# Seven products for two more experts, and a written order of steps: a linear-attention and expert-mix kernel on one core

## The chip, the core and the metric

The kernel runs on one core of a Trainium2 chip. The time is the device time of one execution in microseconds (us), as the median of the runs. A profile is one further execution, taken by the hardware profiler; its rows are in microseconds from the start of the span.

Engines: TensorE (PE in the profile, its weight loads PEld), VectorE (DVE), ScalarE (ACT), GpSimd (POOL), and SyncE (SP), which only issues transfers. GpSimd issues transfers too.

## What is computed

Four sequences (B = 4) of 768 steps, 8 heads of 48. First a linear attention with a decaying state, then a mix of four experts over the 3072 tokens with 8 x 48 = 384 features:

```python
f = 1.0 / (1.0 + np.exp(-f_logit))
for t in range(S):
    state = f[:, :, t, :, None] * state + np.einsum('bhd,bhe->bhde', k[:, :, t], v[:, :, t])
    y[:, :, t] = np.einsum('bhd,bhde->bhe', q[:, :, t], state)
...
p = domain_probs / (domain_probs.sum(-1, keepdims=True) + 1e-09)
for e in range(E):                       # E = 4, w1[e]: 384 x 1024, w2[e]: 1024 x 384
    h = np.maximum(x @ w1[e], 0.0)
    out += p[:, e:e + 1] * (h @ w2[e])
```

## The kernel before

**Chunks and halves.** The 768 steps are cut into six chunks of 128 (c = 0 to 5). A chunk holds 4 x 128 = 512 tokens, four token tiles, one for each batch b. Attention of a chunk runs batch by batch: the gates (`gate1`, `gate2`, ScalarE), the prefix sum of the log gates as a matmul (`cs`, in chunk 0 also `cq`), exponentials (`exps`, `expq`, ScalarE), products with q and k (`q`, `k`, VectorE or GpSimd), transposes (`tpq`, `tpk` on TensorE and their eviction `ev_tp`, or `tp` by DMA), the scores (`at`), masked on their way out of PSUM (`ev_at0`, `ev_at1`; two of them copied by ScalarE and masked by GpSimd, `mask1`), the output (`y`), the state's update (`kv`, `ev_kv`, then four `sf` on GpSimd), and the transposed output as the experts' input (`xt`, `ev_xt`).

**The experts.** In chunk 0 and the first half of chunk 1, experts run one by one over unweighted tokens: `h c.e.fc.n0` is a block of the first matrix product (`mm_h`), `relu` its ReLU, `o c.e.nt.half` half of the second product for a token tile (`mm_o`, L502: 4 matmuls of 384 columns), and `ev_o` adds it, times the token's share p, to the output tile `o` (VectorE, or ScalarE for expert 0). From the second half of chunk 1 on, experts go in pairs over weighted tokens (`hs`, `relu_s`), half a chunk (256 tokens) at a time, and the second product is done with **seven products** in place of eight: each of the three operands is split into 2 x 2 blocks (token tile, half of the 1024, half of the 384 columns), sums of blocks of `h` (`s1` to `s4`, L541) and differences of blocks of `w2` (`t 1`, `t 2`, `t 4` into `ts_sb`, and `t 3` in place, L561) are made on VectorE, and seven block products (`p c.hf.pair.m`, `mm_p`, L574: 8 matmuls of 192 columns each for a pair) are evicted and added into `o` (`ev_p`, 192 columns). Functions for one expert alone exist as well (`add_p1`, L825, `mm_p1`, L583, `s_sum1`, L555, `ev_p1`, L591); `BLOCKED = ()` (L1029) says that no expert uses them.

**Weights and loads.** GpSimd issues the loads of the weights, which are converted to 16 bits on the way, in 11 pieces (`w issue 0` to `w issue 10`): four halves of the first matrices of experts 0 and 1, two halves of expert 0's second matrix, then whole matrices: expert 2's first (6), expert 1's second (7), expert 3's first (8), expert 2's second (9), expert 3's second (10). The last waits for the load of k of chunk 1 (L306). It also issues the loads of v of chunk 0. All other loads, stores and DMA transposes are issued by SyncE in one queue. The loads of f of chunk 1 wait for weight pieces 6 and 8.

**What sets the order.** Every step is an `Op` with a cost for each engine that can run it, a priority, dependencies, and the buffers that it takes and frees (8 PSUM banks among them). `Plan.run` (L92) goes through a modelled time: whenever an engine is free, it takes the step of best priority that is ready then and there; so the plan picks both the order and, where a step has two costs, the engine. `MOVES` (L15) shifts the priorities of 157 steps and pins some of them to an engine. The instructions are then emitted in that order, and on the chip every engine runs its own list in order, waiting on semaphores.

**Fillers.** Where the modelled time leaves TensorE a gap up to the first `h`, matmuls on a constant tile fill it, into a spare PSUM bank that nothing reads (L1011 and L1022):

```python
o.pad, t = int(gap / 0.42) if t < 7.0 else int((gap - 0.5) / 0.25) if gap > PADGAP else 0, o.end
...
for _ in range(o.pad):
    nc.tensor.matmul(out=spare, lhsT=busy[:, 0:128], rhs=busy, start=True, stop=True)
```

In this kernel there are ten: six in front of `cs 0.0`, four in front of the first transposes (`tpk 0.1`).

**The end.** In the last pair of the last half chunk (`TAIL`) products come in an order of their own, so that stores can start early; product 3, the last of the seven as they are set up, is followed by the store of columns 192 to 384 of one token tile.

Of the kernel before, what the change touches and what calls it, by code (L numbers as in the profile page):

```python
# [14 lines left out]
MOVES = (  # L15
    "ld f0.0=-1085.4;ld k0.0=-996.5;ld q0.0=-995;ld f0.1=-1063.1;ld k0.1=-1011.8;ld q0.1=-997;ld f0.2=-1016.8;ld k0.2=-1048.4;"
    "ld q0.2=-166.9;ld q1.2=24.6;expq 0.0=17.8;cs 0.0=-15.3;cq 0.1=51.7;ev_tp 0.1=-2353.3@DVE;cq 0.3=-31.8;cs 0.3=-127.3;"
    "tpq 0.3=51.9;ev_at0 0.2=-26.8;y 0.2=4;ld p=3.1;cs 1.0=11.5;q 1.1=30.5;v 1.1=56.8@POOL;q 1.2=50.2;cs 1.3=270.6;"
    "ev_xt 1.0=136.7@ACT;ev_ys 1.2.1.1=4.6@DVE;ev_at1 1.3=-207.2;y 1.3=51.7;sf 1.0.2=13;sf 1.0.3=26.9;ld f2.0=-181.4;ld k2.2=8.7;"
    "ld q2.2=14.3;h 0.1.3.0=45.1;relu 0.1.3.0=-71.4@DVE;o 0.0.2.0=34;ev_o 0.0.2=-57.7@DVE;h 0.2.2.0=48.5;o 0.1.1.0=31.2;"  # L20
    "o 0.1.2.0=56.8;h 0.2.6.0=186.9;h 0.3.1.0=69.5;o 0.2.0.1=61.7;o 0.2.1.0=88.9;h 0.3.4.0=93.3;o 0.2.3.0=70.7;ev_at0 2.1=-7.7;"
    "ev_at1 2.1=-87.3;ev_ys 2.1.1.0=129.8@ACT;ev_at1 2.3=121.4;ld f3.0=-26.9;ld k3.0=0.1;ld f3.2=21.5;ld q3.2=20;o 0.3.0.0=50.1;"
    "o 0.3.1.1=16.7;o 0.3.3.0=-27.2;o 0.3.3.1=95;store 0.3.0=69.5;h 1.0.3.0=3.1;h 1.1.2.0=49;h 1.2.3.0=37.5;o 1.1.1.1=63.6;"
    "h 1.2.4.0=53.4;h 1.2.5.0=37.4;h 1.2.6.0=-29.2;o 1.2.0.0=200.4;h 1.3.1.0=57.8;h 1.3.2.0=67.2;store 1.0.0=14.5;"
    "hs 1.1.0.0.6=35.5;s3 1.1.0=243.4;s4 1.1.0=217.3;hs 1.1.1.0.0=175.5;ev_at0 3.1=-16.6;kv 3.0=99.1;ev_kv 3.1=47.6;ld f4.2=12;"
    "ld k4.2=23.5;hs 2.0.0.0.0=9.8;p 1.1.1.1=2.1;hs 2.0.0.0.2=-36.6;relu_s 2.0.0.0.2=-20.8@DVE;p 1.1.1.6=5.4;hs 2.0.0.1.2=-24.8;"
    "ev_p 1.1.1.7=144.7;store 1.2.0=28.9;s1 2.0.0=96.7;s3 2.0.0=-259.2;hs 2.0.1.0.0=200.7;hs 2.0.1.1.0=-150.7;hs 2.0.1.0.2=9.8;"
    "relu_s 2.0.1.1.2=-62.7;hs 2.1.0.1.4=3.4;p 2.0.1.3=4;store 2.1.0=51.8;s2 2.1.0=24.1;p 2.1.0.2=159;ev_p 2.1.0.6=-167.6@DVE;"
    "hs 2.1.1.0.4=263.3;tp 4.0=22.8;cs 4.1=7.4;tp 4.2=66.2;ev_at1 4.0=69.6;y 4.1=27.9;ev_ys 4.1.1.0=101.9@DVE;ev_kv 4.3=7.7;"
    "ld f5.0=27.4;ld q5.0=202.1;ld v5.0=-19.4;ld k5.2=-47.3;p 2.1.1.1=11.5;p 3.0.1.1=16.2;hs 3.1.0.1.0=11.7;p 3.0.1.2=7.9;"  # L30
    "s2 3.1.0=75.8;s3 3.1.0=-2.8;hs 3.1.1.1.0=28.1;hs 3.1.1.0.2=26.6;hs 3.1.1.1.2=7.1;hs 3.1.1.0.6=17.4;p 3.1.0.4=88.2;"
    "hs 3.1.1.1.6=-14.6;cs 5.2=10.5;cs 5.3=83.5;at 5.3=22.9;hs 4.0.0.0.0=134.5;p 3.1.1.1=27.9;p 3.1.1.5=117.6;p 3.1.1.4=5;"
    "s1 4.0.0=1.2;hs 4.0.1.0.0=55.6;hs 4.0.1.1.0=171.1;hs 4.0.1.1.2=-25.1;p 4.0.0.5=76.5;hs 4.0.1.0.4=-17.7;hs 4.1.0.1.2=30.5;"
    "p 4.0.1.5=11.3;hs 4.1.1.0.2=39.4;hs 5.0.0.1.0=207.4;ev_p 4.1.1.5=-27.2;hs 5.0.0.1.4=109.2;hs 5.0.1.1.2=46.5;hs 5.0.1.0.4=11.8;"
    "hs 5.0.1.1.4=19.4;hs 5.0.1.0.6=-25.9;p 5.0.0.4=30.3;p 5.0.1.6=542.6;hs 5.1.0.1.2=33.6;p 5.0.1.5=26.4;s1 5.1.0=41.9;"
    "hs 5.1.1.0.0=32.3;hs 5.1.1.1.2=28.8;hs 5.1.1.0.4=85.1;p 5.1.0.7=87.1;p 5.1.1.2=890.3"
)


class Op:  # L40


    def __init__(self, name, costs, emit, prio, deps=(), takes=(), frees=(), lag=0.0):
        self.name, self.costs, self.emit, self.prio = name, costs, emit, prio
        self.deps = [d for d in deps if d is not None]
        self.takes, self.frees, self.lag = list(takes), list(frees), lag
        if name.split(" ")[-1].startswith("0.") and {"ACT", "DVE"} & set(costs):
            self.lag += 0.1
        self.end = self.start = self.engine = None
        self.pad = 0  # L50
        self.port, self.turn = False, None


class Plan:
# [4 lines left out]
    def __init__(self, rooms):  # L59
        self.moves = dict(m.split("=") for m in MOVES.split(";") if m)  # L60
# [3 lines left out]
    def add(self, *args, **kw):  # L64
        op = Op(*args, **kw)
        by, _, engine = self.moves.get(op.name, "0").partition("@")
        op.prio += float(by)
        if engine:
            op.costs = {engine: op.costs[engine]}
        op.port = op.name[0] in "qkvs" and op.name[:2] not in ("kv", "st") and "issue" not in op.name or op.name[:2] == "t "  # L70
        self.ops.append(op)
# [20 lines left out]
    def run(self):  # L92
        for o in self.ops:
            for k in o.frees:
                self.left[k] = self.left.get(k, 0) + 1
        left = sorted(self.ops, key=lambda o: o.prio)
        free_at = {e: 0.0 for o in left for e in o.costs}
        free_at.update({"DMA": 0.8, "DVE": 5.0, "POOL": 3.5, "ACT": 2.1, "PE": 2.0})
        freeing, done, now, port = [], [], 0.0, 0.0
        while left:  # L100
            for f in [f for f in freeing if f[0] <= now + 1e-9]:
                freeing.remove(f)
                self.rooms[f[1]].append(f[2])
            for e in ("PE", "ACT", "DVE", "POOL", "DMA"):
                while free_at[e] <= now + 1e-9:
                    for o in left:
                        if e in o.costs:
                            t = self.ready(o, e)
                            if t is not None and t <= now + 1e-9 and self.take(o):
                                break  # L110
                    else:
                        break
                    left.remove(o)
                    o.engine, o.start = e, now
# [4 lines left out]
                    for k in o.frees:  # L119
                        self.left[k] -= 1  # L120
                        if self.left[k] == 0:
                            freeing.append((o.end + self.LATENCY + (o.lag if e == "DMA" else 0.0), k[0], self.slot[k]))
                    done.append(o)
            nexts = [t for t in free_at.values()] + [f[0] for f in freeing]
            for o in left:
                for e in o.costs:
                    nexts.append(self.ready(o, e) or 0.0)
            nexts = [t for t in nexts if t > now + 1e-9]
            if left and not nexts:
                raise RuntimeError("no step can run: " + ", ".join(o.name for o in left[:8]))  # L130
            if left:
                now = min(nexts)
# [4 lines left out]
def kernel(  # L137
# [95 lines left out]
    for nm, a in (("f", f_logit), ("q", q), ("k", k), ("v", v)):  # L233
# [7 lines left out]
        "ys": ([T, 2, HD], BF16), "xT": ([128, KD, NT], BF16), "xs": ([128, 2, KD, TH], BF16),  # L241
# [7 lines left out]
    alias = {"xT": "x", "xs": "x", "hs": "h", "ys": "yb", "praw": "o"}  # L249
# [51 lines left out]
    def load_w(i, e, which, ks, cols):  # L301
# [4 lines left out]
        if i == w_last:  # L306
# [254 lines left out]
    def t_sum(e, j):  # L561
        b = lambda kh, cols: w2_sb[:, e, half_k(kh), cols]
        t = lambda i: ts_sb[:, e, i - 1]
        o, in0, in1 = {1: (t(1), b(0, HI_), b(0, LO_)), 2: (t(2), b(1, HI_), t(1)), 4: (t(3), b(1, LO_), t(2)),
                       3: (b(0, HI_), b(1, HI_), b(0, HI_))}[j]
        return nc.vector.tensor_tensor(out=o, in0=in0, in1=in1, op=ALU.subtract)

    def factors(m, e, blk, s):
# [3 lines left out]
                7: lambda: (s(3), w(0, HI_))}[m]()  # L572

    def mm_p(c, hf, p, m, bank, first):  # L574
        out_ = tl("mp", c, hf, p, bank)[:, 0:DH]
# [388 lines left out]

    for e in BLOCKED:
        t_sums(e)
# [104 lines left out]
```

## Time and profile before

| | |
|---|---|
| median of 3 runs | 287.11 us (286.66 to 287.74) |
| profiled execution | 287.44 us, of it 285.7 us span |
| TensorE busy | 277.4 us, 3016 matmuls |
| VectorE, ScalarE, GpSimd busy | 196.1, 180.6, 114.1 us |
| transfers | 41.85 MB, mean 146 GB/s |

The span goes from the first to the last instruction; the execution's own time is 1.7 us longer. Matmuls are pipelined: the length printed for a group holds the drain of its last one, so the price of one is taken from the start of a group to the start of the next. A busy row in the view by stretches gives start and end, length, then busy time and number of instructions of TensorE, its weight loads, VectorE, ScalarE and GpSimd, then the granted TensorE clock, the busy share of the DMA engines and GB/s.

### The profile page before, as it was taken

What the parts mean: (1) busy time and instruction counts of PE and PEld (TensorE: products, weight loads), DVE (VectorE), ACT (ScalarE), POOL (GpSimd) and SP (SyncE); (2) the same over time, 40 slices, a digit from 0 to 9 for tenths busy, and PEclk for the clock granted to TensorE, in tenths of its full rate; (3) what the DMA queues carried; (4) which work ended last, traced back from release to release, by engine and by line L of the source; (5) the groups of instructions that cost most, each with busy time, mean ns of one, the idle gap of its engine ahead of it and who ended that gap; (6) DMA issues with size and microseconds to landing.
All of it is one profiled execution on the core that took longest, in us unless ns stands there. A gap on an engine that the chain in (4) does not pass through costs nothing.

```text
span 285.7 us, 7476 instructions
## 1 busy us (share of the span) xinstructions
PE 277.4 (97%) x3016; PEld 236.7 (83%) x3020; DVE 196.1 (69%) x402; ACT 180.6 (63%) x336; POOL 114.1 (40%) x186
## 2 busy tenths in 40 slices
PE   6889999999999999999999999999999999999995
PEld 4667555657877999999999998999899998999994
DVE  5794144697779896875888848886888730874374
ACT  6768756568657963586668766658638348836710
POOL 5999101528663760866036756343750000000000
PEclk9999999999999999999999999999999999999999
DMA  6999999999977999999879999989675210050003
GB/s 157 214 199 207 208 192 205 178 202 178 183 142 151 160 197 155 210 184 185 178 150 189 164 224 210 144 191 158 74 164 107 57 55 2 19 122 31 2 0 110
DMA packets 153687, 41.85 MB, mean 146 GB/s; under 512 B 144029, under 2 KB 152861, under 8 KB 153653
## 3 DMA queue, kind: packets, MB, share of 16 engines
q1 hardware_dynamic: 142404, 34.66, 65.0%
q0 software_dynamic: 11248, 6.72, 16.3%
q8 instruction: 23, 0.38, 0.6%
q14 instruction: 12, 0.09, 0.1%
HBM read 31.51 MB, written 4.72 MB: 127 GB/s over the span
## 4 chain that ended last, share of the span: by engine, by line
PE 78%; DMA 14%; POOL 5%; SPq 1%; issue 0%; DVE 0%; POOLq 0%
PE ps_m L521 33%; PE ps_m L580 29%; DMA w_sb<-in_moe_w_dram 10%; PE ps_m L504 6%; PE ps_m L489 4%; DMA k<-in_k_dram 4%; POOL w_sb L303 2%; PE ps_m L428 2%; PE ps_m L455 1%; POOL vb L284 1%; PE ps_m L451 1%; PE ps_m L338 1%; PE ps_m L461 1%; POOL AT L432 1%; SPq L290 1%
## 5 line engine op out<-in xcount | busy, mean ns | idle before, releaser
L521 PE MATMUL ps_m<-x,w_sb 128*128 128x256 bf16 x864 | 104.8, 273 | 0.0
L529 ACT ACTIVATE h<-ps_m 128x512 bf16<-128x512 f32 x111 | 66.2, 598 | 46.1 <-PE ps_m L521 38.8
L521 PEld LDWEIGHTS <-w_sb 128*128 128x128 bf16 x864 | 82.9, 98 | 9.4
L580 PEld LDWEIGHTS <-S 128*128 128x128 bf16 x576 | 48.7, 98 | 0.9
L607 DVE TENSOR_TENSOR o<-ps_m,o 128x192 f32<-128x192 f32 x91 | 31.3, 354 | 22.0 <-PE ps_m L580 21.0
L580 PEld LDWEIGHTS <-h 128*128 128x128 bf16 x432 | 36.2, 98 | 0.6
L504 PE MATMUL ps_m<-w_sb,h 128*128 128x384 bf16 x192 | 35.3, 326 | 0.4 <-DMA w_sb<-in_moe_w_dram 0.4
L489 PE MATMUL ps_m<-x,w_sb 128*128 128x128 bf16 (+2 forms) x260 | 34.5, 281 | 0.6 <-DMA w_sb<-in_moe_w_dram 0.4
L411 ACT ACTIVATE yb<-ps_m,pn 128x384 bf16<-128x384 f32 x54 | 28.1, 584 | 7.7 <-PE ps_m L455 6.4
L476 POOL TENSOR_TENSOR Sf<-Sf,egs 48x192 f32<-48x192 f32 x40 | 21.0, 526 | 27.1 <-DVE Sf L468 17.4
L444 DVE TENSOR_TENSOR AT<-ps_m,mask 128x512 bf16<-128x512 f32 x40 | 25.2, 683 | 8.6 <-PE ps_m L428 8.5
L500 ACT ACTIVATE h<-ps_m 128x512 bf16<-128x512 f32 (+1 forms) x42 | 22.5, 536 | 12.8 <-PE ps_m L489 11.8
L489 PEld LDWEIGHTS <-w_sb 128*128 128x128 bf16 x264 | 21.7, 98 | 9.5 <-DMA w_sb<-in_moe_w_dram 0.6
L544 DVE TENSOR_TENSOR S<-h 128x1024 bf16<-128x1024 bf16 x36 | 25.2, 713 | 6.1 <-ACT h L529 5.5
L580 PE MATMUL ps_m<-ts_sb,S 128*128 128x192 bf16 x288 | 29.2, 246 | 0.0
L580 PE MATMUL ps_m<-w_sb,S 128*128 128x192 bf16 x288 | 28.7, 246 | 0.0
L504 PEld LDWEIGHTS <-h 128*128 128x128 bf16 x192 | 18.3, 98 | 12.5 <-DMA w_sb<-in_moe_w_dram 0.9
L388 POOL TENSOR_TENSOR qk<-q,e 128x384 bf16<-128x384 f32 x19 | 22.7, 1205 | 14.5 <-ACT e L371 9.7
L580 PE MATMUL ps_m<-w_sb,h 128*128 128x192 bf16 x288 | 28.0, 246 | 0.0
L527 DVE TENSOR_SCALAR h<-ps_m 128x512 bf16<-128x512 f32 x33 | 22.4, 691 | 8.1 <-PE ps_m L521 7.5
L371 ACT ACTIVATE e<-ps_m 128x384 f32<-128x384 f32 x40 | 23.4, 704 | 5.8 <-PE ps_m L338 5.4
L388 POOL TENSOR_TENSOR qk<-k,e 128x384 bf16<-128x384 f32 x20 | 20.2, 1016 | 16.7 <-PE ps_m L580 7.4
(87 smaller groups left out, 317.5 us busy)
## 6 DMA issues: line engine op xcount, KB each, us to landing
out_dram<-o SPq DMA_DIRECT2D x23, 192.0 KB, 2.3
w_sb<-in_moe_w_dram POOLq DMA_DIRECT2D x5, 768.0 KB, 16.3
k<-in_k_dram SPq DMA_DIRECT2D x10, 384.0 KB, 5.6
q<-in_q_dram SPq DMA_DIRECT2D x10, 384.0 KB, 5.2
v<-in_v_dram SPq DMA_DIRECT2D x10, 384.0 KB, 5.4
f<-in_f_logit_dram SPq DMA_DIRECT2D x9, 384.0 KB, 4.6
w_sb<-in_moe_w_dram POOLq DMA_DIRECT2D x6, 384.0 KB, 8.6
f<-in_f_logit_dram SPq DMA_DIRECT2D x6, 192.0 KB, 3.7
```

The lines of the kernel that those rows point to most:

```text
L371: nc.scalar.activation(out=o, in_=i, func=AF.Exp, scale=1.0 if j else -1.0)
L388: return engines[eng].tensor_tensor(out=tl("qk", c, b)[:, j, :, 0:D].rearrange("t (i r) d -> t i r d", r=2), in0=tl("qk"[j], c, b // 2)[:, ...
L411: nc.scalar.activation(out=ys, in_=y, func=AF.Copy, scale=pe)
L444: nc.vector.tensor_tensor(out=tl("AT", c, b)[:, r].rearrange("s i t -> s (i t)"), in0=tl("A", c, b, r).rearrange("s i t -> s (i t)"), in1= ...
L489: nc.tensor.matmul(out=hp(c, e, fc, n0, n1, nf)[:, f], lhsT=w1_sb[:, e, kk, (fc + f) * 128:(fc + f + 1) * 128], rhs=tl("xT", c)[:, kk, n0: ...
L500: nc.scalar.activation(out=dst, in_=src, func=AF.Relu)
L504: nc.tensor.matmul(out=tl("op", c, e, nt)[:, 0:Din], lhsT=tl("h", c, e, half_of(c, nt * T))[:, fc, nt * T:(nt + 1) * T], rhs=w2_sb[:, e, f ...
L521: nc.tensor.matmul(out=out_[:, f], lhsT=w1_sb[:, e, kk, (fc + f) * 128:(fc + f + 1) * 128], rhs=tl("xs", c, hf, p)[:, el, kk, :], start=(k ...
L529: nc.scalar.activation(out=dst, in_=tl("hp", c, hf, p, el, fc), func=AF.Relu)
L544: return nc.vector.tensor_tensor(out=o, in0=in0, in1=in1, op=op)
L580: nc.tensor.matmul(out=out_, lhsT=lhs[:, f, :], rhs=rhs[:, f, :], start=(first and el == 0 and f == 0), stop=(el == 1 and f == KH - 1), sk ...
L607: nc.vector.tensor_tensor(out=o, in0=src, in1=o, op=ALU.add)
```

## The change

Three things are done.

1. `BLOCKED = ((0, 1), (0, 1))`: in chunk 0 (all four token tiles) and in the first half of chunk 1, experts 0 and 1 use the seven products for one expert in place of `o`/`ev_o`. Their `t` sums are made before chunk 0's experts; experts 2 and 3 keep the direct form there. (A further buffer, `t3`, is for experts that would use the form in only one of the two places; there is none.)
2. The last weight piece (expert 3's second matrix) is loaded in two halves, 10 and 11, both behind the load of k of chunk 1. Product 3 of the last pair is done in two halves of 96 columns, each with its own eviction and store.
3. `MOVES` and the choice by priority are gone. `STEPS` lists the steps of each engine by number; `Plan.run` takes them strictly in that order, each as soon as it is ready in the modelled time, which still gives the buffers and the fillers. Steps that could run on two engines are bound by the list they stand in.

```diff
-MOVES = (
...
+STEPS = {
+    "PE": (
+        "72 70 63 61 77 90 76 88 68 67 99 98 156 81 79 95 104 131 94 111 86 85 106 101 113 100 137 269 124 267 127 118 143 129 271 120 "
...
+                    for o in seq[e][:1] if STEPS else seq[e]:
+                        t = self.ready(o, e)
...
-        if i == w_last:
+        if i >= w_late:
             after(ins["w", i], ins[1, "k", 0])
...
-    pieces += [(e, which, every, every) for e, which in ((2, 1), (1, 2), (3, 1), (2, 2), (3, 2))]
-    w_last, w_gate = len(pieces) - 1, len(pieces) - 3
+    pieces += [(e, which, every, every) for e, which in ((2, 1), (1, 2), (3, 1), (2, 2))]
+    w_late, w_gate = len(pieces), len(pieces) - 2
+    pieces += [(3, 2, slice(i * KF // 2, (i + 1) * KF // 2), every) for i in range(2)]
...
-        if e in BLOCKED:
+        if e in BLOCKED[c]:
             tps = sorted({nt // 2 for nt in nts})
             return [lambda i=i: add_p1(c, e, tps, i) for i in range(7)]
...
+            if (pg, m) == (TAIL, 3):
+                half = DH // 2
+                for n0 in (0, half):
+                    mm = P.add(f"p {c}.{hf}.{p}.{m}.{n0}", {"PE": 0.34}, lambda _, n0=n0: mm_p(c, hf, p, m, bank, first, slice(n0, n0 + half)),
+                               pr + 0.01 * n0, deps=d, takes=[key], lag=0.2, frees=[("S", c, hf, p, sk)])
+                    c0 = cols * DH + n0
+                    ev = P.add(f"ev_p {c}.{hf}.{p}.{m}.{n0}", {"DVE": 0.27}, lambda g, c0=c0: ev_p(c, hf, p, bank, r, slice(c0, c0 + half), g, False),
+                               pr - 1, deps=[mm, evp[c, hf, r, cols]], takes=[("o", c, hf)], frees=[key])
+                    add_store(c, 2 * hf + r, c0, c0 + half, pr, [ev])
+                return
...
-BLOCKED = ()
+BLOCKED = ((0, 1), (0, 1))
```

In the built programs the start of TensorE's list reads, in steps (a number in brackets is that many fillers; `0.b` is batch b of chunk 0):

```text
before: [6] cs 0.0, cq 0.0, cs 0.1, cq 0.1, [4] tpk 0.1, cq 0.2, tpk 0.0, cs 0.2, tpq 0.0, tpq 0.1, at 0.0, tpq 0.2, at 0.1, cs 0.3, cq 0.3, tpk 0.2, y 0.0, kv 0.0, at 0.2, xt 0.0, y 0.1, tpk 0.3, tpq 0.3, pp, kv 0.1, h 0.0.0.0
after:  [6] cs 0.1, cq 0.1, [1] cs 0.0, cq 0.0, tpk 0.1, cs 0.3, tpq 0.1, cq 0.3, tpk 0.0, tpq 0.0, at 0.1, at 0.0, [39] pp, cs 0.2, cq 0.2, tpk 0.3, y 0.0, kv 0.0, [8] tpq 0.3, y 0.1, tpk 0.2, tpq 0.2, xt 0.0, at 0.3, xt 0.1, at 0.2, kv 0.1, h 0.0.0.128
```

(`pp` transposes the experts' shares, which `ld p` loads.) SyncE's first loads, and GpSimd's first steps:

```text
SyncE before:  f0.0 f0.1 k0.2 f0.2 k0.1 k0.0 q0.0 q0.1 q0.2 f0.3 k0.3 q0.3 p
SyncE after:   f0.1 f0.0 f0.3 k0.0 k0.1 q0.1 k0.2 q0.0 k0.3 f0.2 p q0.3 q0.2
GpSimd after:  v issue 0, 1, 2, w issue 0, v issue 3, k 0.3, w issue 1, mask1 0.1, w issue 2, 3, 4, 5, mask1 0.2, w issue 6, sf 0.1.0, sf 0.1.1, sf 0.0.0, sf 0.0.1, sf 0.2.0, w issue 7, sf 0.1.2, sf 0.3.0, w issue 8, w issue 9, w issue 10, w issue 11
```

## The prediction

> **What bounds the kernel now.** I read the busy shares first, then the busy time of each stretch, then the TensorE timeline of the first 32 us, and last the chain of waits.
>
> ```profile
> PE 277.4 (97%) x3016; PEld 236.7 (83%) x3020; DVE 196.1 (69%) x402; ACT 180.6 (63%) x336; POOL 114.1 (40%) x186
> ```
>
> ```profile
> 0.00:5.00 5.00, 2.74 (x6) 0.89 (x7) 3.60 (x13) 2.32 (x4) 3.75 (x17) 1.00 0.52 120
> 5.00:12.00 7.00, 6.37 (x64) 5.00 (x63) 3.17 (x7) 5.35 (x15) 4.39 (x5) 1.00 1.25 230
> 12.00:18.20 6.20, 4.68 (x78) 3.70 (x77) 6.14 (x13) 3.93 (x10) 6.09 (x8) 1.00 1.70 195
> 18.20:26.00 7.80, 7.75 (x140) 7.17 (x142) 5.23 (x16) 6.26 (x12) 7.56 (x15) 1.00 1.27 205
> 26.00:58.00 32.00, 31.84 (x189) 17.33 (x190) 13.67 (x23) 20.42 (x34) 8.11 (x14) 1.00 1.18 198
> 58.00:64.00 6.00, 5.63 (x67) 3.66 (x67) 5.33 (x12) 3.41 (x7) 1.25 (x3) 1.00 0.96 192
> 64.00:272.00 208.00, 208.00 (x2358) 188.79 (x2357) 150.83 (x304) 137.31 (x256) 83.00 (x128) 1.00 0.75 137
> 272.00:286.00 14.00, 10.37 (x125) 10.11 (x122) 8.10 (x20) 1.55 (x4) 0.00 (x0) 0.98 0.16 56
> ```
>
> The second number of a row is the stretch's length, the third is TensorE's busy time. From 64 to 272 us TensorE never stops, so every microsecond put into its queue, or taken out, is a microsecond of span. It is idle only before 18 us, while attention of chunk 0 is built up, for about 0.4 us near 58, and after its last matmul. That matmul ends at 272.48 + 9.91 = 282.39 us (chain of waits, below); the 3.3 us to the span's end are one DVE addition, a store and its landing.
>
> ```profile
> 1.52 2.74 PE L1022 MATMUL ps_m<-S 128*128 128x512 bf16 x6 [1.52 <-DVE S L185]
> ...
> 7.79 1.62 PE L1022 MATMUL ps_m<-S 128*128 128x512 bf16 x4
> 9.25 0.39 PE L397 MATMUL ps_m<-ident,qk 128*128 128x128 bf16 x4
> ...
> 30.50 1.46 PE L489 MATMUL ps_m<-x,w_sb 128*128 128x512 bf16 x6
> 31.79 0.49 PE L504 MATMUL ps_m<-w_sb,h 128*128 128x384 bf16 x2
> ```
>
> L1022 are the filler matmuls, which compute nothing that is kept. The printed length of a group holds the last matmul's drain, so the price of one is taken from start to start: a 512-column matmul costs (31.79 - 30.50)/6 = 0.215 us once TensorE runs at its full pace; the six fillers at 1.52 us took 2.74/6 = 0.46 each, the four at 7.79 (9.25 - 7.79)/4 = 0.37.
>
> ```profile
> 48.32 10.26 DMA w_sb<-in_moe_w_dram
> ...
> 70.14 2.60 PE ps_m L504 x16
> ...
> 160.44 1.32 PE ps_m L580 x16
> ...
> 272.48 9.91 PE ps_m L580 x120
> ```
>
> A 384-column matmul of the direct second product (L504) costs 2.60/16 = 0.1625 us, a 192-column one of the seven products (L580) 1.32/16 = 0.0825.
>
> **The change, part by part.**
>
> *Seven products.* For one expert in chunk 0 the direct form is 4 token tiles x 8 = 32 matmuls x 0.1625 = 5.20 us; seven products are 7 x 2 x 4 = 56 x 0.0825 = 4.62, so 0.58 less. Two experts in chunk 0 and, at half the tokens, two in chunk 1: 2 x 0.58 + 2 x 0.29 = **-1.74 us**. Bounds: 0 (if the one-expert form gains nothing) and -1.74.
>
> *What it adds elsewhere.* VectorE gets 16 S sums (eight at the 0.71 us of the L544 row, eight of half the size, about 0.45) and 31 of the 42 added evictions at 0.36 (L607 row), and loses eight of L511/L515 at 0.61: 5.7 + 3.6 + 11.2 - 4.9 = +15.6 us. Between 26 and 64 us VectorE is busy 13.67 + 5.33 = 19.0 of 38 us, so there is room; if that cover fails, the next product on the same bank waits for an eviction, a few tenths each time. Later the list also moves 17 more ReLUs of `hs` from ScalarE to VectorE, 17 x 0.69 = 11.7 us on top of 150.83 in 208: still under 80%.
>
> *The written order, and the fillers.* The rule at L1011 puts fillers where the list has a gap, once, when the program is built. In the instruction lists of the two programs there are 10 before (6 + 4) and 54 after: 6 at the start, 1 between the batches' prefix sums, **39 in one block** behind `at 0.0` and in front of `pp` and `cs 0.2`, 8 in front of `tpq 0.3`. TensorE's queue is in order, so they run whether there is a gap on the chip or not. Behind the 39 stand `pp`, `cs 0.2`, `cq 0.2`, `tpk 0.3`, `y 0.0`, `kv 0.0`, and so everything ScalarE, VectorE and GpSimd make of batch 2's prefix sum, and the first `h`. The block costs 39 x 0.215 = 8.4 us, the eight 1.7.
>
> Would TensorE have waited there anyway? `cs 0.2` needs `ld f0.2`, now tenth on SyncE's queue. All of SyncE's loads for chunk 0 are 192 KB but for the small `ld p`, so places can be exchanged: the tenth landed at 11.51 us before (it was `f0.3`; ScalarE took it at 11.53 and had both gates done at 12.6). So `cs 0.2` could start near 12.7, and `ld p`, the eleventh, lands about a microsecond later. When does the block start? `q 0.0` is eighth (the eighth landed at 9.85), 0.5 us product on VectorE, 0.2 transposes and 0.2 hand-over, 0.69 eviction: `at 0.0` starts near 11.6, as it did before (11.63), and ends near **12.0**. So at most some 2 us of the block lie in a wait that was there already; the rest is added.
>
> *The sum.* TensorE's work from 12.0 us on, before: 4.68 + 7.75 + 31.84 + 5.63 + 208.00 + 10.37 = 268.3 us, with 282.39 - 12.0 - 268.3 = 2.1 idle in between. At the same point the new list has the same steps behind it (`cs`/`cq 0.3` in place of `0.2`) and also `at 0.1`, 0.33. So
> 12.0 + 268.3 - 0.3 - 1.74 + 47 x 0.215 (10.1) = 288.3 us, the end of TensorE without any wait.
> To this comes the idle time after 12 us: less than the 2.1 of before, since the fillers now let loads and evictions get ahead; I take 1.0, with 0 and 5 as ends (5 is some twenty waits of a quarter microsecond, or one late weight). And the end, 3.3, as before: the last matmul group is `p 5.0.1.4` in both lists. 288.3 + 1.0 + 3.3 = **292.6 us of span**, 6.9 more. The profiled execution had 287.44 us for 285.7 of span; the median 287.11 stands 1.4 above that span. 292.6 + 1.4 = **294.0 us**.
>
> *Last product in halves.* 16 matmuls of 96 columns for 8 of 192. Four of 96 columns (L461) took 19.84 - 19.68 = 0.16 us, 0.04 each: 0.64 against 0.66, nothing. Its smaller store is not the last one: store 5.1.0, behind `p 5.0.1.4`, is last on SyncE's queue before and after. Bounds -0.2 and +0.3.
>
> *GpSimd's queue and the weights.* Six weight pieces keep their place, roughly. Piece 6 (expert 2's first weights) now stands behind `mask1 0.2`, which waits for `at 0.2` behind both blocks of fillers: 12.0 + 8.4 = 20.4, then about 2.0 of TensorE steps, 1.7 of fillers, 2.0 to the end of `at 0.2` = 26.1, ScalarE 0.7, mask 0.65, issue 0.8: about 28.3, where it was 18.89. Alone on the queue it lands some 7 us later, at 35; TensorE wants it after 16 units of `h` (0.645 each), 4 products and 1.5 us of attention from about 26.5, at 41. Pieces 7 to 9 stand behind state updates, issued from 34 to 38; piece 8 lands near 45, piece 9 some 5 later (before: 40.64 and 45.58), wanted by `o 0.2.1` near 26.5 + 27 x 0.645 + 12 x 0.66 + 1.5 = 53. Expert 3's second weights wait for `ld k1.0`, which landed 7.1 us after piece 8 before: 52, plus the 10.26 of the chain for both halves: 62, wanted at about 65. So all are covered, the last by 3 us; what is later than that is added one for one.
>
> On the fillers the Trainium skill speaks for the change: "TensorE: Matmul & The Clock Gate", Part 1, says that a matmul runs at half rate until TensorE has been busy for some 3.4 us, and again after an idle window of that length, so a wait filled with matmuls keeps the pace. The trace agrees in the ramp (0.46 us a filler at 1.5 us, 0.215 later), but shows no idle stretch of 3 us behind 5 us that would need filling.
>
> **The rivals.**
>
> (a) *A late operand behind the new order* (weights through GpSimd's queue, or evictions on a fuller VectorE). For it: covers of 3 us where before GpSimd issued piece 9 at 22.6. Against: the DMA engines get 10 us of start, and VectorE is at half load there. Price 2 to 5 us: 296 to 299, about 297.
>
> (b) *The fillers start at the slow pace.* Before, the slow pace lasted from 1.5 to some point in 7.8 to 9.25 us, about 7 us. The new list has waits of a few tenths up to 1 us ahead of the block. If another stretch of 3.5 to 7 us passes at 0.43, 8 to 16 fillers cost 0.215 more each: +1.7 to +3.5, 295.7 to 297.5, about 296.5.
>
> (c) *The other side: fillers are nearly free.* They share one stationary tile and one output bank and wait for nothing. If one cost what a 128-column matmul costs (L489, twelve from 23.13 to 23.80, 0.056 us), 47 of them would be 2.6 instead of 10.1, and the time 286.5. It turns at 6.9 us less, a filler of (10.1 - 6.9)/47 = 0.068 us. Against it: the ten fillers of the trace took 0.37 to 0.46 each, and 512-column matmuls with work in them 0.215.
>
> (d) *A filler half way between these rows*, (0.056 + 0.215)/2 = 0.135 us: 47 x 0.08 = 3.8 less, 290.2. Against it the same rows. The same page of the Trainium skill, section "Back-to-back issue gap", speaks for such a price: it gives about 131 ns for 512-column matmuls in a stream with weight loads, where this trace shows 215.
>
> (e) *The seven products do not save*: +1.7, 295.7.
>
> **How the numbers follow.** Forecast 0.66, its own range 292.9 to 295.3 (idle 0 to 2.2, start of the block 0.3 either way); (a) 0.14; (b) 0.08; (e) 0.04; (d) 0.03; (c) 0.04, and 0.01 for what I do not see. The range 291.5 to 298.5 leaves out (c), (d) and the far part of (a), under 2 in 10 together. About 0.5% (1.4 us) is what these runs can tell from no change. Faster than that needs (c) in full: 0.03; within it 0.02; slower 0.95.
>
> **What would show it.** Right: one block of 39 fillers from about 12 to 20.4 us at 0.215 each; first `h` near 26.5 to 27.5 instead of 18.18; TensorE then dense, about 1.7 us less of L504 and L580 together; last matmul near 289. Wrong: a filler far from 0.215; a wait of a microsecond or more on DMA or VectorE behind 30 us (a); a busy sum of TensorE other than 277.4 - 1.7 + 9 = 285.

## The result, and the profile after

| | median, us | from, to | runs | profiled execution | its span |
|---|---|---|---|---|---|
| before | 287.34 | 286.66, 287.74 | 4 | 287.44 | 285.7 |
| changed | 295.24 | 294.57, 296.01 | 4 | 296.01 | 294.3 |

The changed kernel takes 1.0278 times as long (95% interval 1.0241 to 1.0315): 7.9 us more. 294.0 was forecast, with 291.5 to 298.5 as its range.

The first line of the changed kernel's page, busy time by engine:

```profile
PE 285.3 (97%) x3136; PEld 246.0 (84%) x3144; DVE 219.2 (74%) x464; ACT 161.2 (55%) x318; POOL 111.7 (38%) x190
```

TensorE is busy for 285.3 us where it was 277.4. Where the added time stands, the TensorE timeline of the changed kernel shows (start, length, line, operation, count; in brackets the wait before it):

```profile
11.91 0.40 PE L474 MATMUL ps_m<-QK 48*128 48x128 bf16 x8 [0.28 <-DVE QK L325]
12.48 8.37 PE L1087 MATMUL ps_m<-S 128*128 128x512 bf16 x38 [0.16 <-issue]
20.77 0.66 PE L361 MATMUL ps_m<-ident,o 24*128 24x24 f32 x4
21.36 0.50 PE L388 MATMUL ps_m<-gp,Up 128*128 128x192 bf16 x4
...
22.95 1.67 PE L1087 MATMUL ps_m<-S 128*128 128x512 bf16 x7
24.46 0.39 PE L443 MATMUL ps_m<-ident,qk 128*128 128x128 bf16 x4
...
27.39 0.78 PE L535 MATMUL ps_m<-x,w_sb 128*128 128x128 bf16 x11
```

The first filler of each block has no matmul record in the trace. Its weight load has one, and the weight loads (PEld) are 39 and 8, as in the program:

```profile
12.25 8.10 PEld L1087 LDWEIGHTS <-S 128*128 128x128 bf16 x39
...
22.69 1.44 PEld L1087 LDWEIGHTS <-S 128*128 128x128 bf16 x8
```

So from 12.25 to 20.77 TensorE runs fillers and nothing else, and eight more follow from 22.69 to 24.46. 8.52 us for 39 are 0.218 each. The first `h` (L535 here) stands at 27.39, where it was at 18.18 before:

```profile
18.18 0.84 PE L489 MATMUL ps_m<-x,w_sb 128*128 128x128 bf16 x12 [0.41 <-DMA w_sb<-in_moe_w_dram]
```

The windows of the changed kernel, cut where the timeline turns (length, then TensorE's busy time):

```profile
12.48:27.39 14.91, 14.30 (x123) 8.25 (x124) 4.71 (x10) 4.98 (x12) 5.72 (x8) 1.00 1.39 192
27.39:64.00 36.61, 36.31 (x358) 26.34 (x361) 32.00 (x71) 20.37 (x40) 11.93 (x19) 1.00 0.95 160
64.00:90.00 26.00, 25.95 (x290) 21.22 (x289) 22.54 (x53) 18.39 (x43) 15.02 (x24) 1.00 1.05 196
90.00:102.00 12.00, 10.13 (x97) 7.12 (x94) 8.51 (x17) 7.00 (x13) 7.28 (x17) 1.00 0.99 145
102.00:281.00 179.00, 179.00 (x2082) 166.85 (x2080) 136.05 (x276) 101.69 (x194) 63.81 (x104) 1.00 0.67 129
```

TensorE's idle time is the difference of the two numbers: 0.61, 0.30, 0.05, **1.87** and 0. While the fillers run, ScalarE is busy for 4.98 and VectorE for 4.71 of 14.91 us: the others wait for what stands behind the block. The 1.87 us near 95 us are new, since before TensorE never stopped from 64 us on. The list of TensorE's waits names them:

```profile
PE ps_m L474 <- DMA QK<-qk: 1.3, 1, 1.3
...
PE ps_m L501 <- POOL vb L325: 0.5, 1, 0.5
```

One transposing transfer of chunk 2's products with q and k (1.3 us) and one conversion of v on GpSimd (0.5 us) come late. At the end nothing changed: the last entry of the chain of waits is

```profile
281.69 9.27 PE ps_m L626 x120
```

so the last matmul ends at 290.96, 3.3 us before the span's end, as before.

### The profile page after: what moved, and what is told of

It is laid out like the page before. It is cut to its first block, busy times and chain, and to the rows that moved or that the text cites. A ratio compares the mean times of both kernels' runs of the same rounds, so it can differ in the third digit from the quotient of the medians.

```text
span 294.3 us, 7772 instructions
## 1 busy us (share of the span) xinstructions
PE 285.3 (97%) x3136; PEld 246.0 (84%) x3144; DVE 219.2 (74%) x464; ACT 161.2 (55%) x318; POOL 111.7 (38%) x190
## 4 chain that ended last, share of the span: by engine, by line
PE 88%; POOL 4%; DMA 4%; DVE 2%; issue 1%; ACT 0%; SPq 0%; POOLq 0%; DVEq 0%
PE ps_m L567 31%; PE ps_m L626 28%; PE ps_m L535 8%; PE ps_m L550 4%; PE ps_m L1087 4%; PE ps_m L635 3%; DMA egs<-e 2%; PE ps_m L474 2%; DMA k<-in_k_dram 2%; PE ps_m L501 1%; PE ps_m L507 1%; PE ps_m L497 1%; POOL qk L434 1%; PE ps_m L443 1%; PE ps_m L384 1%
## 5 line engine op out<-in xcount | busy, mean ns | idle before, releaser
L567 PE MATMUL ps_m<-x,w_sb 128*128 128x256 bf16 x864 | 107.4, 273 | 0.0
L575 ACT ACTIVATE h<-ps_m 128x512 bf16<-128x512 f32 x94 | 54.1, 601 | 40.2 <-PE ps_m L567 38.3
L654 DVE TENSOR_TENSOR o<-ps_m,o 128x192 f32<-128x192 f32 (+1 forms) x92 | 30.5, 350 | 18.3 <-PE ps_m L626 16.6
L573 DVE TENSOR_SCALAR h<-ps_m 128x512 bf16<-128x512 f32 x50 | 33.7, 685 | 9.5 <-PE ps_m L567 9.3
L457 ACT ACTIVATE yb<-ps_m,pn 128x384 bf16<-128x384 f32 x55 | 29.7, 586 | 17.0 <-issue 7.0
L626 PEld LDWEIGHTS <-h 128*128 128x128 bf16 x432 | 36.6, 98 | 1.1
L535 PE MATMUL ps_m<-x,w_sb 128*128 128x128 bf16 (+2 forms) x258 | 35.8, 280 | 0.3
L626 PE MATMUL ps_m<-w_sb,S 128*128 128x192 bf16 (+1 forms) x296 | 29.0, 244 | 0.0
L546 ACT ACTIVATE h<-ps_m 128x512 bf16<-128x512 f32 (+1 forms) x43 | 19.7, 493 | 15.0 <-PE ps_m L535 14.1
L535 PEld LDWEIGHTS <-w_sb 128*128 128x128 bf16 x264 | 21.5, 98 | 7.4 <-issue 0.2
L434 POOL TENSOR_TENSOR qk<-k,e 128x384 bf16<-128x384 f32 x20 | 20.3, 1022 | 17.8 <-PE ps_m L507 10.5
L514 DVE TENSOR_TENSOR Sf<-Sf,ps_m 48x192 f32<-48x192 f32 x40 | 14.0, 349 | 6.3 <-PE ps_m L507 5.6
L550 PE MATMUL ps_m<-w_sb,h 128*128 128x384 bf16 x96 | 18.1, 326 | 0.0
```

The costliest lines, as they stand in the source:

```text
L434: return engines[eng].tensor_tensor(out=tl("qk", c, b)[:, j, :, 0:D].rearrange("t (i r) d -> t i r d", r=2), in0=tl("qk"[j], c, b // 2)[:, ...
L457: nc.scalar.activation(out=ys, in_=y, func=AF.Copy, scale=pe)
L535: nc.tensor.matmul(out=hp(c, e, fc, n0, n1, nf)[:, f], lhsT=w1_sb[:, e, kk, (fc + f) * 128:(fc + f + 1) * 128], rhs=tl("xT", c)[:, kk, n0: ...
L550: nc.tensor.matmul(out=tl("op", c, e, nt)[:, 0:Din], lhsT=tl("h", c, e, half_of(c, nt * T))[:, fc, nt * T:(nt + 1) * T], rhs=w2_sb[:, e, f ...
L567: nc.tensor.matmul(out=out_[:, f], lhsT=w1_sb[:, e, kk, (fc + f) * 128:(fc + f + 1) * 128], rhs=tl("xs", c, hf, p)[:, el, kk, :], start=(k ...
L573: nc.vector.tensor_relu(out=dst, in_=tl("hp", c, hf, p, el, fc))
```

## The experiments

All are compared with the kernel before on the same chip. Times are medians, with the lowest and highest run; a ratio is to the kernel before with its 95% interval. Before had 287.46 us beside experiments 1, 2, 3 and 5, 287.72 beside 4, 6, 7 and 8, and 287.71 beside 9 to 11; these three groups ran on different chips, and the changed kernel's 295.24 was measured separately. The theory: the 47 late fillers make the whole loss, since the written list has gaps only in the model of the builder, and what else was changed is a gain of about the products' 1.7 us. Rivals: TensorE needs the fillers to keep its pace; the reordered queues make the loss.

**1. The changed kernel without late fillers** (`e1_nofill`).

```diff
-            o.pad, t = int(gap / 0.42) if t < 7.0 else int((gap - 0.5) / 0.25) if gap > PADGAP else 0, o.end
+            o.pad, t = int(gap / 0.42) if t < 7.0 else 0, o.end
```

> The changed kernel with its first 7 fillers only; the block of 39 and the 8 are left out, all orders kept. Theory (the block of fillers is the loss): in the changed kernel ld f0.2 landed at 12.43 us, both gates take 1.06, so cs 0.2 starts near 13.6 in place of 21.36; from there to the first h it was 6.03 us with 1.5 of fillers, so the first h starts near 18.1 to 19.5 in place of 27.39, and the time is 295.2 - 8 to 9 = about 286.7 us (285.5 to 288). Rival 1 (the fillers keep TensorE's pace): the waits from 12.3 to 18 us let TensorE fall back to 0.43 us a 512-column matmul for some us, first h blocks twice as long, 288 to 291. Rival 2 (the written order as a whole is the loss, the fillers only fill waits): first h still near 25 or later, time above 292.

285.96 us (285.65 to 286.35, 10 runs), ratio 0.9937 (0.9913 to 0.9962). The timeline at the place of the block:

```profile
12.79 0.63 PE L361 MATMUL ps_m<-ident,o 24*128 24x24 f32 x4 [0.34 <-DMA o<-in_moe_domain_probs_dram]
13.50 0.49 PE L388 MATMUL ps_m<-gp,Up 128*128 128x192 bf16 x4
...
18.39 0.78 PE L535 MATMUL ps_m<-x,w_sb 128*128 128x128 bf16 x11
```

The step that stood behind the block (L361) starts at 12.79 after a wait of 0.34 us, not at 20.77: nearly nothing of the 8.5 us lay in a wait that was there. The first `h` comes 9.0 us earlier, and the time is 9.3 us less; both rivals had 288 us or more. What is left of the change is a gain of 0.6%.

**2. The same fillers in the kernel before** (`e2_before_fill`), 39 in front of `tpq 0.2` and 8 in front of `xt 0.0`.

```diff
+        o.pad = {"tpq 0.2": 39, "xt 0.0": 8}.get(o.name, o.pad)
```

> The kernel before with 39 fillers put in front of tpq 0.2 (behind at 0.0, where TensorE stands at 12.1 us) and 8 in front of xt 0.0; nothing else. Theory (a filler costs 0.213 us of TensorE's queue and little of it falls into waits): 47 x 0.213 = 10.0, less the 2.1 us that TensorE is idle between 12 and 64 us: +8 to +10, time 295 to 297.5 us. Rival (the weights' arrival paces the first 60 us, so a late start is made up): under +5, time below 292.5.

295.44 us (294.98 to 295.77, 4 runs), ratio 1.0262 (1.0215 to 1.0309). The block in its timeline:

```profile
12.16 8.37 PE L1023 MATMUL ps_m<-S 128*128 128x512 bf16 x38 [0.16 <-issue]
```

The fillers by themselves, with no other edit, cost 8.0 us.

**3. The same count of fillers, 128 columns wide** (`e4_short_fill`), in the changed kernel. Only the width of the 47 late fillers is another; their number and place are the same.

> The changed kernel with all 54 fillers, but the 47 behind 7 us are 128 columns wide in place of 512. Theory (fillers are work like any other, priced by their columns): 47 x 0.056 = 2.6 in place of 10.0 us; the block ends near 14.7, cs 0.2 starts there, first h near 20 to 20.5, time 295.2 - 7 = about 288.2 us (287 to 289.5). Rival (what delays is the number of fillers or the place of the block, not the columns): time above 291.

287.49 us (287.11 to 288.52, 10 runs), ratio 0.9991 (0.9962 to 1.0019).

```profile
12.23 2.35 PE L1088 MATMUL ps_m<-S 128*128 128x128 bf16 x39
14.52 0.66 PE L361 MATMUL ps_m<-ident,o 24*128 24x24 f32 x4
```

39 take 2.29 us from start to start, 0.059 each: 6.2 us less than in the changed kernel, and the eight later ones 1.3 less (0.45 us for 1.77). The time is 7.8 us less, so the loss goes with what the fillers take, not with their number.

**4. Where the fillers come from** (`e5_list_only`). In the list of transfers that the builder's model walks, four loads move forward. SyncE's own queue is the same to the instruction; nothing else is edited.

```diff
-        "3 0 7 1 4 5 8 2 10 13 15 6 17 19 21 23 155 25 27 11 9 29 31 ...
+        "3 0 7 1 4 5 8 2 10 6 155 11 9 13 15 17 19 21 23 25 27 29 31 ...
```

> The changed kernel with four numbers moved in one list: ld f0.2, ld p, ld q0.3 and ld q0.2 stand directly behind ld k0.3 in the list of transfers, ahead of the entries for v and the weights, which SyncE does not issue. The order that SyncE gets is the same to the instruction; only the modelled time of these four loads is earlier, so the modelled gaps and with them the 39 and the 8 fillers are gone (the 7 at the start stay; some PSUM banks change). Theory (the fillers came from the model's single file of transfers and are all of the loss): as e1_nofill, 285.96 us, within 0.5. Rival (the loss has a second part in the written order of loads): above 288 us.

286.6 us (285.25 to 287.44, 12 runs), ratio 0.9945 (0.9916 to 0.9974). That is 0.64 above experiment 1, which ran on another chip; the ratios of the two are alike (0.9945 and 0.9937). The program then has 7 fillers instead of 54, and this is what its timeline shows where the block stood:

```profile
12.09 0.41 PE L473 MATMUL ps_m<-QK 48*128 48x128 bf16 x8 [0.45 <-DVE QK L324]
13.36 0.63 PE L360 MATMUL ps_m<-ident,o 24*128 24x24 f32 x4 [0.86 <-DMA o<-in_moe_domain_probs_dram]
```

The model sends SyncE's and GpSimd's transfers through one file, so `ld f0.2` (6), behind the v loads of GpSimd (13, 15), came late in the model alone, and the rule at L1076 filled a gap of which the chip has little: the wait there is 0.86 us in this trace and 0.34 in experiment 1's.

**5. The wait near 95 us** (`e3_k2_early`): in the changed kernel `ld k2.0` (260) goes in front of `ld f2.2` (263), past two transposing transfers and a store.

```diff
-... 261 263 194 201 506 260 266 ...
+... 261 260 263 194 201 506 266 ...
```

> The changed kernel with one step moved on SyncE's queue: ld k2.0 goes in front of ld f2.2, tp 1.2, tp 1.3 and store 0.2.0 in place of behind them. Theory (TensorE's 1.8 us of waits near 95 us come from k of chunk 2 landing at 85.48, which holds GpSimd's products and so the transposes tp 2.0, 2.1): the waits between 90 and 102 us fall under 0.5 us, time 1.3 to 1.8 less, about 293.7 us. Rival (egs 1.1, whose landing GpSimd waits 4.2 us for, holds the same place anyway): under 0.5 us less, 294.7 or more.

294.56 us (294.52 to 294.79, 6 runs), ratio 1.0234 (1.0196 to 1.0272), 0.68 less than the changed kernel. Its window and wait at the same place:

```profile
90.00:102.00 12.00, 11.30 (x119) 8.29 (x116) 8.62 (x18) 7.53 (x15) 8.09 (x17) 1.00 1.06 161
```

```profile
PE ps_m L468 <- DMA QK<-qk: 0.7, 1, 0.7
```

1.17 of the 1.87 us are gone. 0.68 of it shows in the medians, between the two expectations, and 1.3 in the ratios; the two intervals overlap. The late `k` is part of that wait, and GpSimd's late conversion went with it. Why the transposes still land 0.7 us late is open: in the changed kernel the transfer issued at 86.67 landed at 89.69 and the one issued at 89.31 at 95.61; here the later one was issued at 88.6 and still took 6.4 us to land.

**6. Both edits** (`e6_nofill_k2`, experiments 1 and 5 together), and later the same kernel again beside the runs of 9 to 11 (`e12_again`).

> e1_nofill and e3_k2_early together: no fillers behind 7 us and ld k2.0 in front of ld f2.2. e1_nofill's TensorE is idle 0.66 us between 90 and 102 us, where e3_k2_early cut 1.87 to 0.70. Theory (that idle time goes with the load): 0.3 to 0.6 us less than e1_nofill, about 285.5 us. Rival (a value cast on GpSimd, which TensorE waited 0.7 us for, ends there last whatever k does): 285.7 to 286.2, no difference.

> The version without late fillers and with the earlier load of k for chunk 2 once more, as the measure for the other three on the same chip: 285.5 to 286.4, 0.4 to 1.0 per cent below the kernel before. Rival: its lead was the chip's noise, within 0.3 per cent of the kernel before.

285.96 us (284.96 to 286.9, 12 runs), ratio 0.9917 (0.9883 to 0.9951), then 285.98 (285.03 to 287.28, 12 runs), 0.9927 (0.9897 to 0.9957). TensorE is without a pause from 64 to 102 us in both. It beats the kernel before by 0.8%; against experiment 1 no difference can be told, as the rival had it.

**7. The seven products undone** (`e7_direct`): experiment 1's kernel with the direct second product for the two experts in chunk 0 and in chunk 1's first half, 96 matmuls of 384 columns for 168 of 192.

```diff
-BLOCKED = ((0, 1), (0, 1))
+BLOCKED = ((), ())
```

> e1_nofill with the seven products of chunk 0 and of chunk 1's first half undone: the direct steps o stand at the places of the products, ev_o at places of their evictions, the S sums are gone, t 0.3 and t 1.3 follow the last direct use. Theory (TensorE-bound, 0.0825 against 0.1625 us a matmul): 1.74 us more than e1_nofill, 287.7 us (287.3 to 288.1). Rival 1 (the one-expert form gains nothing because VectorE gets 15 us of work): no more than 0.5 us above e1_nofill. Rival 2 (the gain of e1_nofill over before has another source): at or below 286.

287.56 us (286.53 to 288.64, 12 runs), ratio 0.998 (0.9951 to 1.0009). That is 0.96 more than experiment 4 and 1.6 more than experiment 6 on the same chip; the interval of a ratio is about 0.8 us to either side. It just touches that of experiment 6 and overlaps that of experiment 4. So the products are worth something near the 1.74 by the medians, and a closer number the runs don't give. (The direct steps stand at the places of the products, in a list that was written for those.)

**8. The halves undone** (`e8_whole`): experiment 1's kernel with expert 3's last weights in one transfer and the last product in one piece.

```diff
+    pieces[-2:] = [(3, 2, every, every)]
...
-            if (pg, m) == (TAIL, 3):
+            if False:
...
-                    done_ = {2: [(0, 0, DH)], 7: [(1, 0, Din)]}
+                    done_ = {2: [(0, 0, DH)], 7: [(1, 0, Din)], 3: [(0, DH, Din)]}
```

> e1_nofill with the halves undone: expert 3's second weights in one load, the last pair's product 3 in one piece of 192 columns with one eviction and one store. Theory (halves are worth nothing: the last store is another one, and the weights have 3 us of cover): within 0.4 us of e1_nofill, 285.6 to 286.4 us. Rival (the weights in one piece are late as they were before, 0.4 us near 58): 286.3 to 286.7 with a wait on w_sb in the trace.

287.82 us (286.89 to 288.75, 12 runs), ratio 0.9987 (0.996 to 1.0013): 1.2 us more than experiment 4 and about 1.9 more than experiment 6 (which also has the earlier `k`), above both expectations, where the prediction had put the halves at nothing. Two waits appear:

```profile
PE ps_m L549 <- DMA w_sb<-in_moe_w_dram: 1.1, 1, 1.1
...
PE ps_m L500 <- DMA vb<-in_v_dram: 0.8, 1, 0.8
```

The second, on a load of v, is not explained, and the traces of 9 and 10 don't have it.

**9 and 10. One half at a time**, in experiment 6's kernel: the last product whole (`e9_tail_whole`), the last weights whole (`e10_weights_whole`). The edits are the lines shown under 8, the first for the weights, the others for the product.

> The version without late fillers and with the earlier load of k for chunk 2 (285.96), with one part undone: the last product in one piece of 192 columns, its store too; the last weights stay in halves. Theory: the halves of the last product are worth nothing (16 matmuls of 96 columns at 0.04 us for 8 of 192 at 0.0825), so 285.5 to 286.4, and the tail behind the last matmul stays at 3.2 to 3.4 us. Rival: part of the 1.9 us that undoing both halves cost lies in the tail: 286.6 to 287.2.

> The same version with the other part undone: expert 3's last weights in one transfer, the last product in halves. Theory: the whole transfer lands too late once TensorE is not held back by the fillers, and a direct second product waits about 1.1 us for it: 286.8 to 287.8, with a wait of TensorE on the weights (w_sb) of 0.8 to 1.5 us between 20 and 64 us. Rival: the wait is absorbed by later ones, 285.5 to 286.4.

| kernel | median, us | from, to (12 runs each) | ratio |
|---|---|---|---|
| both in halves (`e12_again`) | 285.98 | 285.03, 287.28 | 0.9927 (0.9897 to 0.9957) |
| product whole | 286.72 | 285.91, 287.55 | 0.9943 (0.9911 to 0.9975) |
| weights whole | 287.44 | 286.66, 289.2 | 0.9978 (0.9946 to 1.0011) |

By the medians the product's halves are worth 0.7 us, but the intervals of the ratios overlap, and it is the traces that decide against the theory of a worthless split. The chains of the two kernels end, product whole first,

```profile
270.98 9.25 PE ps_m L625 x112
```

```profile
270.73 9.28 PE ps_m L625 x120
```

at 280.23 and 280.01 us, while the spans are 284.1 and 283.3: the tail behind the last matmul is 3.9 us against 3.3. (Experiment 8, product whole too, has 3.8; all the others of these kernels, with halves, have 3.3 to 3.4.) The cause stands on SyncE's queue (product whole, then in halves):

```profile
275.23 6.21 SPq L657 DMA_DIRECT2D out_dram<-o  x6
```

```profile
274.98 5.82 SPq L657 DMA_DIRECT2D out_dram<-o  x7
```

The last store is issued by 281.44 and by 280.80. An issue takes some 0.4 us of SyncE; with the product whole, its store is issued late and the last ones queue behind it. TensorE's price for the 16 or 8 matmuls had nothing to do with it. The kernel before has the product whole as well and a tail of 3.3, so the 0.6 us are a price of the whole product in the new order of steps, which the halves take away again.

The weights' halves are worth 1.5 us by the medians, of which the waits of TensorE show half (the rest is open):

```profile
PE ps_m L549 <- DMA w_sb<-in_moe_w_dram: 0.8, 1, 0.8
```

In halves the weights landed at 56.17 and 58.85, whole at 59.02. The direct product begins with the first half, so it can start 2.9 us sooner. In the changed kernel itself, where everything from the first `h` on is 9 us later, they landed at 64.71 and 67.47 and no wait for them shows. That doesn't make the halves idle there. TensorE's order is the same in both kernels, and in experiment 10 the wait for these weights stands 4 matmuls into the group that reads in the changed kernel

```profile
65.43 2.77 PE L550 MATMUL ps_m<-w_sb,h 128*128 128x384 bf16 x16
```

so it uses them first at 65.43 + 4 x 0.1625 = 66.08, between the two landings. In experiment 10 the whole transfer landed 0.2 us behind the second half of `e12_again` (59.02 for 58.85). In the changed kernel it would by this estimate land near 67.6 and be waited for some 1.5 us; this was not run.

**11. No filler at all** (`e11_no_filler`), not even the seven before 7 us, otherwise experiment 6's kernel.

```diff
-            o.pad, t = int(gap / 0.42) if t < 7.0 else 0, o.end
+            o.pad, t = 0, o.end
```

> The same version without any filler, also without the seven before 7 us. Theory: the pace of TensorE rises some 7 us after its first matmul (in the version with seven fillers a group of four 192-column matmuls takes 0.59 us from start to start at 5.1 and 7.0 us and 0.33 at 9.6); without fillers the first matmul is at 5.1, so the work up to about 12 us runs at the slow pace, some 2 us of work twice as long, part of it in waits: first h 0.5 to 1.5 us later, 286.4 to 287.5. Rival 1: the pace rises about 3.4 us after the first matmul, at 8.5: no change, 285.5 to 286.3. Rival 2: without the lead the slow pace lasts longer, past 18 us: more than 288.

285.65 us (284.65 to 286.4, 11 runs), ratio 0.9902 (0.9871 to 0.9933): no change that can be told from experiment 6. Rival 1 had the number but not the reason: the pace does not rise at 8.5 us, since the four 192-column matmuls at 9.85 still take 0.62 us from start to start. Its windows (the number behind the five engines is the granted clock) show what nobody had expected:

```profile
10.50:13.90 3.40, 1.75 (x29) 1.20 (x26) 2.74 (x5) 2.15 (x6) 3.38 (x4) 0.99 1.54 196
13.90:17.20 3.30, 3.25 (x37) 3.15 (x37) 1.67 (x3) 2.48 (x6) 3.08 (x6) 0.50 1.72 189
17.20:20.50 3.30, 2.78 (x56) 2.31 (x54) 2.52 (x5) 2.49 (x5) 1.50 (x3) 0.99 1.44 199
```

For 3.3 us TensorE's granted clock is 0.50; this is taken up in the last section.

## Why the prediction was right

**Sum.** Forecast: TensorE's end at 288.3, idle time 1.0, tail 3.3, span 292.6, and 1.4 on top. Measured in the profiled execution: the last matmul at 290.96, span 294.3, and a median of 295.24 (the profiled execution, 296.01 us, is the longest of the four, so the terms read from it lie some 0.8 us above the median's). The forecast was 1.24 us low, and its mechanism, the block, is what experiments 1, 2 and 3 show from three sides.

**The fillers.** 39 in one block, 8 later; 0.218 us each in the block, where 0.215 was taken; the 47 took 8.52 + 1.77 = 10.3 us for 10.1. That little of it is given back by waits that were there (at most "some 2 us", and nothing in the sum) held: without them the first `h` comes 9.0 us earlier in experiment 1. At this price rivals (c) and (d) fell. The Trainium skill's page "TensorE: Matmul & The Clock Gate", section "Back-to-back issue gap", gives some 131 ns for 512-column matmuls between weight loads; here they took 218, and 59 at 128 columns where it gives 81.

**Start of the block**: 12.25 for 12.0. `at 0.0` began at 11.91, 0.3 later than assumed.

**Idle time behind 12 us**: this is the term that was mis-sized. 2.8 us (0.61 + 0.30 + 0.05 + 1.87) for 1.0. Two thirds of it lie in one place that the prediction did not look at: it followed GpSimd's weights and SyncE's loads for chunk 0, but not SyncE's queue for chunk 2, where `ld k2.0` stands behind two transposes and a store; moving that load took 1.17 of the 1.87 us away (experiment 5), the rest is open. That is rival (a) in small, with its price of 2 to 5 us nearly reached at its lower end, and not where it had been looked for. The 1.33 us wait on a transfer at 95 us is also one of the signs that the prediction had listed under "Wrong", so it was right on the block and not on what follows it. 0.25 of the start, 0.2 of the fillers and 1.8 of the idle time make 2.2 against the 1.7 by which TensorE's end with the idle time was low; some 0.5 less work than summed stands against it. The forecast's own range, up to 295.3, allowed 2.2 us of idle time. With 2.8 the time still came out at 295.24: that is luck.

**VectorE** got 23.1 us more (219.2 for 196.1), where 15.6 + 11.7 = 27.3 were summed. Behind 5 us no wait of TensorE on it was longer than 0.32 us.

**The weights.** Piece 6 was issued at 28.50 (28.3 forecast) and landed at 36.12 (35), piece 8 at 47.61 (45), piece 9 at 51.47 (50), the last two at 64.71 and 67.47 (62 for both). Each came later than forecast, the last by 5.5 us, and none was waited for. For the last piece that is not the cover of 3 us that the prediction counted on: it landed 1.4 us after TensorE had begun with the first half at 66.08, and the split alone let TensorE begin.

**The seven products.** TensorE busy 285.3 for 285 forecast; a row of 24 of their matmuls in the chain of waits,

```profile
46.54 1.98 PE ps_m L635 x24
```

gives 1.98 / 24 = 0.0825 us each, the price that was used. Experiment 7 puts their worth between 1.0 and 1.6 us by the medians, for 1.74. That speaks against rival (e), and its intervals leave room for less.

**The halves.** "Worth nothing, -0.2 to +0.3" was wrong as a statement on the edit: by the medians the product's are worth 0.7 us (experiment 9) and the weights', without the fillers, 1.5 (experiment 10). For the product the prediction had priced TensorE and looked at which store is last, but not at how long SyncE takes to issue those ahead of it. It did no harm to the sum because the tail was taken as 3.3 from the trace of before, and with the halves it came out as that. For the weights it took both halves to land at 62, in front of their use; by the landings the halves gain in the changed kernel too, up to an estimated 1.5 us. This did no harm to the sum either, since with the halves there is no wait.

**The slow pace, rival (b).** The fillers of the block took 0.218 us on average, so they ran at the full pace. The granted clock of 1.00 in their window would not have shown it: it reads 1.00 in the first 5 us as well, where a filler took 0.46.

**What the change would have been without its fillers**: a gain of 0.6% (experiments 1 and 4), and 0.8% with the earlier `k` of experiment 6. By subtraction the written order by itself costs some of what the products and halves bring: experiment 8, order and products without the halves, stands level with before. That remainder was not run alone.

## What to carry to other kernels

A filler is put where a model has a gap, and runs whether the chip has it or not: in an in-order queue it costs its full length from the moment the gap is only in the model, so count the fillers in the built program and look for the wait that they are to fill in a trace without them. A list that only feeds a model can change the program: here moving four entries that no queue follows took 47 instructions out and 8.6 us off the time. Whether a transfer or a store is worth splitting is decided at the queue that issues it and at the first piece's user, not by the price of the matmuls. A trace of the kernel with the split has no wait that would tell: undo the split, or compare the landing of the last piece with the first use.

## What was not expected of the hardware

**The clock falls without a long pause.** In experiment 11's windows above TensorE is busy for 1.75 of 3.40 us, then the granted clock is 0.50 for 3.3 us, then full again. The timeline there:

```profile
11.93 0.40 PE L473 MATMUL ps_m<-QK 48*128 48x128 bf16 x8 [0.36 <-DVE QK L324]
13.60 0.64 PE L360 MATMUL ps_m<-ident,o 24*128 24x24 f32 x4 [1.26 <-DMA o<-in_moe_domain_probs_dram]
14.29 0.80 PE L387 MATMUL ps_m<-gp,Up 128*128 128x192 bf16 x4
14.88 0.29 PE L391 MATMUL ps_m<-par,gp 128*128 128x2 bf16 x4
```

The longest pause is 1.26 us, and the four matmuls at 14.29 take 0.59 us from start to start; in experiment 1, at 13.50, they took 0.33. The traces of experiments 4, 7 and 10 have the same dip, from 14.05, 14.8 and 13.25 us, after stretches of 3.4 us in which TensorE was busy for 2.02, 2.19 and 2.00 us; the trace of `e12_again`, busy for 2.71 of 3.4 from 10.5 us on, has none. But from 10.1 to 13.5 us experiment 1 was busy for 1.86 us and has no dip, and experiment 7 for 1.15, and its clock fell only 1.3 us later. So busy time alone doesn't decide it, and what does is open. The Trainium skill ("TensorE: Matmul & The Clock Gate", Part 1) has the pace fall after an idle window of some 3.4 us whose start is free-running; the length of the dip agrees, but the window was half busy here, not idle.

Such a dip lowers the mean clock of a run by 3.3 x 0.5 / 285 = 0.006. Of the 105 timed runs of the kernels without late fillers, 55 have a mean clock below 0.9965; of the 24 of the four with the block (the changed one, experiments 2, 3 and 5), none. Where one kernel has both, the medians of the two kinds differ by -0.1 to 1.0 us. Of 92 runs of the kernel before, with ten fillers ahead of 9.3 us, 28 are below 0.9965, and there it costs more: 17 runs near 0.994 have medians 1.1 to 1.5 us above the others of their chip, and 11 near 0.986, twice the drop, 3.1 to 3.3 us. Where in the run those drops stand is not known, since the traced run has none. So fillers do keep the pace here, as they are meant to, but what they prevent is worth about a microsecond or less in half of the runs, and the 512-column ones cost 9. Those of 128 columns kept it too, for 2.7 us.

**The start.** Leaving out the first seven fillers, which run from 1.5 us, cost nothing that the times show. The matmuls with work in them begin at 5.0 us either way. Without the seven they run at the slow pace up to some 10.5 us. With them the full pace is there at 5.0 us in the traces of experiments 1, 7 and 9 (four 192-column matmuls in 0.33 us) and comes between 8.7 and 10.7 us in the others, and the waits for loads that follow take up the difference.
